# Six-layer cross network on one core: tail weights in one broadcast DMA per layer, first group loaded in half chunks with its tails on column tiles, late residual tile transposed in halves

## The chip, the cores and the metric

One core of one Trainium2 chip. Times are device microseconds of one execution. The time of a run is about 1.8 us more than the span of the profile of the same run (477.49 beside 475.7 for the kernel before). All runs told here fell in the fast state, with a granted TensorE clock of 0.994 to 1.000.

## The reference

```python
B, F, D, L = 16384, 26, 16, 6          # Din = 416
def reference(x0, ws, bs):
    x = x0
    for l in range(L):
        proj = jnp.einsum('bd,de->be', x, ws[l]) + bs[l]
        x = x0 * proj + x
    return x
```

x0 is 16384 x 416, ws is 6 x 416 x 416, all in bf16.

## The kernel before

The rows are worked on in eight groups (0 to 7) of 2048, with features on partitions. 416 features are three tiles of 128 and a tail of 32. A group is four chunks of 512 rows; the tails of its four chunks are stacked into one tile of 128 partitions, and their product with the 32 tail rows of a weight matrix is done by row-tiled matmuls (L477 in the profiles), four of which run side by side: eight take 0.61 us at 22.78 in the profile before, eight whole-array ones 1.89 at 12.21. For that the 32 tail rows of each layer's weights lie four times in `w3[l]`.

Every operation goes through `add(engine, instruction, reads, writes, lane)`, which works out the semaphore waits. "sp" is SyncE, whose queue issues nearly all transfers.

```python
def load_w3(l, eng):                                  # tail rows of layer l, once per quarter
    for j in range(NJ):
        add(eng, lambda h, j=j: h.dma_start(w3[l][j * T32:(j + 1) * T32, :], ws[l, NT * P:D, :]), ...)

def load_group(g, between=lambda: None):
    ...
    turn(0)                                           # DMA transposes, one per tile of 128 features
    add("sp", lambda h: h.dma_start_transpose(Tb, x0[rows, D - P:D]), ...)   # the tails' columns
    turn(1)
    turn(2)
    between()                                         # group 1: weights of layer 1
    for j in range(NJ):                               # the "tail rows": four quarters of the tail tile
        add("sp", lambda h, q=q, j=j: h.dma_start(x0s[s][q, XW:XW + CH], Tb[P - T32:P, j * CH:(j + 1) * CH]), ...)
    ...

# ---- start of the SyncE queue
load_nat(0, 0, 2)                                     # group 0 comes row-major, TensorE transposes it
load_nat(0, 2, KK)
load_wm(0, "sp")
for j in range(1, NJ):
    load_nat(j, 0, KK)
load_w3(0, "sp")
load_group(1, lambda: load_wm(1, "sp"))
load_wm(2, "sp")
load_w3(2, "sp")

def transposed_chunk(j):                              # 12 transposes of the three tiles, 4 of the tail
    ...
    for n, (t, k) in enumerate(seq + [(NT, k) for k in range(KK)]):
        ...
        add("pe", lambda h, t=t, k=k, b=b, c=c: h.transpose(
            psum_t(b)[:, c], x0n[:, j, k, first[t]:first[t] + P], ident[:, :]), ...)
    ...                                               # copies out by ScalarE and VectorE

def first_job():
    ...
    transposed_chunk(1)
    transposed_chunk(2)
    full(g, l, 0, ba, True, True, chunks=[1])
    transposed_chunk(3)
    load_w3(1, "act")                                 # from ScalarE's queue
    full(g, l, 1, bb, True, True, chunks=[1])
    full(g, l, 0, ba, True, True, chunks=[2, 3])
    rows32(g, l, 0, ba, False)                        # the first row-tiled matmuls
    ...

def rest_turn(t):                                     # residual of the last layer, tile t, back to row-major
    add("sp", lambda h: h.dma_start_transpose(
        x5f[:, :, t * P:(t + 1) * P], xs[s][:, t * GC:(t + 1) * GC]), ...)
```

Group 7 is written row-major; its last stores, three of 416 KB, one of 208 KB from SyncE and one of 208 KB from ScalarE, end the kernel.

Of the kernel before, what the change touches and what calls it, by code (L numbers as in the profile page):

```python
# [3 lines left out]
P = 128  # L4
CH = 512
# [193 lines left out]
def bass_standalone__cross_network_dcn__recsys_kernel(  # L199
# [56 lines left out]
    def x0_tok(s, t, j):  # L256
        return ("x0", s, t, j)
# [21 lines left out]
    def load_wm(l, eng):  # L279
        add(eng, lambda h: h.dma_start(wm[l][:, :, :], ws[l, 0:NT * P, :].rearrange("(t p) f -> p t f", p=P)),  # L280
            writes=[("wm", l)], lane=f"wm{l}", batch=0)

    def load_w3(l, eng):
        for j in range(NJ):
            add(eng, lambda h, j=j: h.dma_start(w3[l][j * T32:(j + 1) * T32, :], ws[l, NT * P:D, :]),
                writes=[("w3", l, j)], lane=f"w3{l}", batch=0)

    def load_group(g, between=lambda: None):
        s = slot(g)
        rows = slice(g * GC, (g + 1) * GC)  # L290
        def turn(t):
            add("sp", lambda h: h.dma_start_transpose(
                x0s[s][:, t * GC:(t + 1) * GC], x0[rows, t * P:(t + 1) * P]),
                writes=[x0_tok(s, t, j) for j in range(NJ)], lane=f"x0_{s}_{t}", batch=g)

        turn(0)
        add("sp", lambda h: h.dma_start_transpose(Tb, x0[rows, D - P:D]),
            writes=[("ost", t, j) for t in range(NT + 1) for j in range(NJ)], lane="Tb", batch=g)
        turn(1)
        turn(2)  # L300
        between()
        for j in range(NJ):
            q = slice(j * T32, (j + 1) * T32)
            add("sp", lambda h, q=q, j=j: h.dma_start(x0s[s][q, XW:XW + CH], Tb[P - T32:P, j * CH:(j + 1) * CH]),
                reads=[("ost", 0, 0)], writes=[("x03q", s, j)], lane=f"x03_{s}", batch=g)

        if turn_of(g, 1):
            rotate(x0s[s][:, XW:XW + CH], x0s[s][:, XW + CH:XW + 2 * CH], turn_of(g, 1),
                   x03_toks(s), ("x03r", s), f"x03r_{s}", g)
# [210 lines left out]
    def load_nat(j, k0, k1):  # L520
        add("sp", lambda h: h.dma_start(x0n[:, j, k0:k1, :], perm(g0, j)[:, k0:k1, :]),  # L521
            writes=[("nat", j, k) for k in range(k0, k1)], lane=f"nat{j}{k0}", batch=0)
# [6 lines left out]
    load_nat(0, 2, KK)  # L529
    load_wm(0, "sp")  # L530
    for j in range(1, NJ):
        load_nat(j, 0, KK)
    load_w3(0, "sp")
    load_group(1, lambda: load_wm(1, "sp"))
    load_wm(2, "sp")
    load_w3(2, "sp")

# [8 lines left out]
    def psum_t(b):  # L546
        return psum[:, b * CH:(b + 1) * CH].bitcast(BF16)

    def transposed_chunk(j):
        ba, bb = ((0, 1), (3, 0), (1, 3), (0, 1))[j]  # L550
        s = slot(0)
        first = (0, P, 2 * P, D - P)
        seq = [(t, k) for t in range(NT) for k in range(KK)]
        if j == 0:
            seq = [(t, k) for k2 in (0, 2) for t in range(NT) for k in (k2, k2 + 1)]
        for n, (t, k) in enumerate(seq + [(NT, k) for k in range(KK)]):
            if j == 0 and n == NT * 2:
                keep_busy(2, 3)
            b, o = (ba, t * CH) if t < 2 else (bb, (t - 2) * CH)
            c = slice(o + k * P, o + (k + 1) * P)  # L560
            add("pe", lambda h, t=t, k=k, b=b, c=c: h.transpose(  # L561
                psum_t(b)[:, c], x0n[:, j, k, first[t]:first[t] + P], ident[:, :]),
                reads=[("nat", j, k), x0_tok(nat, 0, 0), "ident"], writes=[("ps", b)])
        for t in range(2):
            add("act", lambda h, t=t: h.activation(  # L565
                x0s[s][:, cols(t, j)], psum_t(ba)[:, t * CH:(t + 1) * CH], ACT_F.Copy),
                reads=[("ps", ba)], writes=[x0_tok(s, t, j)])
        add("dve", lambda h: h.tensor_copy(x0s[s][:, cols(2, j)], psum_t(bb)[:, 0:CH]),  # L568
            reads=[("ps", bb)], writes=[x0_tok(s, 2, j)])
        q = slice(j * T32, (j + 1) * T32)  # L570
        add("dve", lambda h: h.tensor_copy(x0s[s][q, XW:XW + CH], psum_t(bb)[P - T32:P, CH:2 * CH]),
            reads=[("ps", bb)], writes=[("x03q", s, j)])

    def first_job():

        g, l = 0, 0
        start_job(g, l)
        transposed_chunk(0)
        bt = 7
        for t in range(NT):  # L580
            add("pe", lambda h, t=t: h.transpose(
                psum_t(bt)[:, t * 8:t * 8 + L], brow[0:L, t * P:(t + 1) * P], ident[0:L, 0:L]),
                reads=["brow", "ident"], writes=[("ps", bt)])
        for j in range(NJ):
            q = slice(j * T32, (j + 1) * T32)
            add("pe", lambda h, j=j, q=q: h.matmul(
                psum_t(bt)[q, NT * 8:NT * 8 + L], brow[0:L, NT * P:D], ident[0:L, 0:L],
                is_transpose=True, tile_position=(0, j * T32)),
                reads=["brow", "ident"], writes=[("ps", bt)])
        add("act", lambda h: h.activation(  # L590
            bias[:, :, :], psum_t(bt)[:, 0:32].rearrange("p (t l) -> p t l", l=8)[:, :, 0:L], ACT_F.Copy),
            reads=[("ps", bt)], writes=["bias"])
        keep_busy(8, 3)
        ba, bb = [4, 5, 6, 7], [2, 3, 0, 1]
        full(g, l, 0, ba, True, True, chunks=[0])
        full(g, l, 1, bb, True, True, chunks=[0])
        transposed_chunk(1)
        transposed_chunk(2)
        full(g, l, 0, ba, True, True, chunks=[1])
        transposed_chunk(3)  # L600
        load_w3(1, "act")
        full(g, l, 1, bb, True, True, chunks=[1])
        full(g, l, 0, ba, True, True, chunks=[2, 3])
        rows32(g, l, 0, ba, False)
        evacuate(g, l, 0, ba, [0, 1], 2, vector=[2, 3])
        full(g, l, 1, bb, True, True, chunks=[2, 3])
        rows32(g, l, 1, bb, False)
        rows32(g, l, 2, ba, True)
        evacuate(g, l, 1, bb, list(range(NJ)), 2)
        full(g, l, 2, ba, False, True, lambda j: evacuate(g, l, 2, ba, [j], 1))  # L610
        finish_tile(g, l, NT)
        tails([(g, l)])
# [66 lines left out]
    def rest_turn(t):  # L679

        s = xset[(LAST, L - 1)]
        if t == 0:
            add("pool", lambda h: h.memset(warm[:, :], 0.0), writes=x0_all(s5) + x03_toks(s5) + ["x5 free"])
        add("sp", lambda h: h.dma_start_transpose(
            x5f[:, :, t * P:(t + 1) * P], xs[s][:, t * GC:(t + 1) * GC]),
            reads=[("x", s, t, j) for j in range(NJ)] + ["x5 free"],
            writes=[("x5n", j, t) for j in range(NJ)], lane=f"x5_{t}", batch=0)

    items = []
    where = {(b[min(1, len(b) - 1)], 0): b for b in batches[:-1]}  # L690
# [263 lines left out]
```

## Time and profile before

| | before |
|---|---|
| time, median of 3 runs | 477.13 us (476.96 to 477.26) |
| span of the profiled execution | 475.7 us (that execution took 477.49) |
| TensorE busy | 97% |
| granted clock | 0.999 |

How to read what the prediction shows: the first of its fences is the part "engines" of the page (busy us, share of the span, instructions) with the last line of the part "chain that ended last". The second is a timeline: start and length in us, engine, line, operation, output and inputs, shapes, count, and in brackets the idle time before the group with what released it. The third are waits: engine, output, line, releaser, then the total, the number and the longest.

### The profile page before, as it was taken

Reading aid. Unit: us, or ns where it says so; the run is one execution under the profiler, and the core shown is the slowest. Engines: PE = TensorE matmul, PEld = TensorE weight load, DVE = VectorE, ACT = ScalarE, POOL = GpSimd, SP = SyncE. Lnnn points to the kernel's source line nnn. Section 1 sums busy time; section 2 is a strip of 40 time slices with the busy share of each in tenths; the row PEclk is TensorE's granted clock in tenths of the full one; section 3 lists DMA queues with packets and bytes.
Section 4 is the critical chain, followed back from the end, with each engine's and each line's share of the span. In section 5 each row is a group of like instructions: output and inputs, shape, how many; then the busy total and the mean of one; then the engine's idle time right before and its main releaser. Section 6 shows DMA issues by size and latency. Waiting matters only on the chain.

```text
span 475.7 us, 8355 instructions
## 1 busy us (share of the span) xinstructions
PE 462.2 (97%) x3325; PEld 195.7 (41%) x3379; DVE 404.0 (85%) x696; ACT 342.4 (72%) x372; POOL 6.8 (1%) x15
## 2 busy tenths in 40 slices
PE   7999999999999999999999999999999999999995
PEld 6344444444444444444444444434444444444442
DVE  2888888888888888898889869988888888888896
ACT  4677777777777777777777777777777777777785
POOL 1000000000000000000000000000000000000000
PEclk9999999999999999999999999999999999999999
DMA  8866950640002397369308940990000039025899
GB/s 223 181 150 137 190 113 1 142 81 1 28 7 44 63 228 158 76 139 244 84 21 195 208 108 9 178 279 2 1 10 25 4 64 242 15 45 117 227 155 288
DMA packets 138363, 53.31 MB, mean 112 GB/s; under 512 B 112330, under 2 KB 137428, under 8 KB 138324
## 3 DMA queue, kind: packets, MB, share of 16 engines
q1 hardware_dynamic: 137848, 52.46, 49.2%
q8 instruction: 26, 0.43, 0.4%
q10 hardware_dynamic: 476, 0.32, 0.2%
q14 instruction: 13, 0.11, 0.1%
HBM read 5.97 MB, written 13.63 MB: 41 GB/s over the span
## 4 chain that ended last, share of the span: by engine, by line
PE 95%; issue 1%; DMA 1%; ACT 1%; DVE 1%; SPq 0%
PE ps L456 77%; PE ps L477 7%; PE ps L497 6%; PE ps L798 2%; DMA x<-in_x_dram 1%; PE ps L471 1%; ACT tw L394 1%; PE ps L561 1%; PE ps L488 1%; DVE x L864 0%; PE ps L809 0%; ACT x L852 0%; DVE x L858 0%; PE ps L841 0%; SPq L521 0%
## 5 line engine op out<-in xcount | busy, mean ns | idle before, releaser
L394 ACT ACTIVATE tw<-ps,bias 128x1024 bf16<-128x1024 f32 (+1 forms) x295 | 299.8, 1071 | 119.8 <-PE ps L477 80.7
L456 PE MATMUL ps<-x,wm 128*128 128x512 bf16 x1638 | 371.7, 379 | 5.8 <-issue 3.7
L456 PEld LDWEIGHTS ps<-x,wm 128*128 128x128 bf16 x1692 | 158.9, 98 | 213.5 <-issue 27.9
L403 DVE TENSOR_TENSOR tw<-tw,x 128x1024 bf16<-128x1024 bf16 (+1 forms) x285 | 192.3, 682 | 52.8 <-ACT tw L394 52.4
L408 DVE TENSOR_TENSOR x<-tw,x 128x1024 bf16<-128x1024 bf16 (+1 forms) x285 | 183.0, 682 | 0.0
L477 PE MATMUL ps<-x,w 32*128 32x512 bf16 x512 | 39.2, 379 | 0.0
L497 PE MATMUL ps<-x,wm 128*32 128x512 bf16 x564 | 33.0, 380 | 0.0
L434 ACT ACTIVATE ts<-ps,bias 128x512 bf16<-128x512 f32 x47 | 28.8, 701 | 0.0
L438 DVE TENSOR_TENSOR x<-ts,x 128x512 bf16<-128x512 bf16 x47 | 18.6, 417 | 3.7 <-DMA x<-x 3.6
L497 PEld LDWEIGHTS ps<-x,wm 128*32 128x32 bf16 x564 | 13.8, 96 | 17.6 <-issue 5.3
L477 PEld LDWEIGHTS ps<-x,w 32*128 32x128 bf16 x512 | 7.8, 92 | 27.6 <-issue 27.1
L436 DVE TENSOR_TENSOR ts<-ts,x 128x512 bf16<-128x512 bf16 x47 | 18.5, 417 | 0.0
L666 POOL COPY ost<-ot 128x512 bf16<-128x512 bf16 x6 | 5.4, 898 | 423.7 <-DMA ot<-x 423.7
L798 PE MATMUL ps<-wm,x 128*128 128x416 bf16 x48 | 9.5, 340 | 0.0
L852 ACT ACTIVATE x<-ps 128x416 bf16<-128x416 f32 x16 | 7.7, 533 | 2.0 <-PE ps L798 1.9
L568 DVE COPY x<-ps 128x512 bf16<-128x512 bf16 x4 | 1.7, 424 | 8.7 <-PE ps L561 8.7
L565 ACT ACTIVATE x<-ps 128x512 bf16<-128x512 bf16 x8 | 4.3, 594 | 5.6 <-PE ps L561 5.6
L798 PEld LDWEIGHTS ps<-wm,x 128*128 128x128 bf16 x48 | 4.3, 98 | 4.2 <-issue 1.0
L561 PE MATMUL ps<-ident,x 128*128 128x128 bf16 x64 | 4.6, 226 | 1.4 <-DMA x<-in_x_dram 0.9
L858 DVE TENSOR_TENSOR x<-x,x 128x832 bf16<-128x832 bf16 (+1 forms) x10 | 5.0, 504 | 1.1 <-ACT x L852 1.1
L488 PE MATMUL ps<-x,w 32*32 32x512 bf16 x188 | 5.9, 374 | 0.0
L471 PE MATMUL ps<-x,w 32*32 32x512 bf16 x208 | 5.6, 385 | 0.0
(38 smaller groups left out, 35.7 us busy)
## 6 DMA issues: line engine op xcount, KB each, us to landing
out_dram<-ost SPq DMA_DIRECT2D x6, 1664.0 KB, 7.1
x<-in_x_dram SPq DMA_DIRECT2D x7, 416.0 KB, 8.0
x<-x SPq DMA_DIRECT2D x24, 96.0 KB, 2.2
wm<-in_ws_dram SPq DMA_DIRECT2D x6, 312.0 KB, 3.7
out_dram<-ost SPq DMA_DIRECT2D x2, 832.0 KB, 6.7
x<-x SPq DMA_DIRECT2D x22, 64.0 KB, 2.0
out_dram<-x SPq DMA_DIRECT2D x3, 416.0 KB, 3.6
x<-ost SPq DMA_DIRECT2D x28, 32.0 KB, 2.2
```

The lines of the kernel that those rows point to most:

```text
L394: add("act", lambda h, a=a, w=w, b0=b0: h.activation(tw[r][:, a * CH:(a + w) * CH], psum[:, b0 * CH:(b0 + w) * CH], ACT_F.Identity, bias=b ...
L403: add("dve", lambda h, a=a, e=e: h.tensor_tensor(tw[r][:, a * CH:e * CH], tw[r][:, a * CH:e * CH], x0s[s0][:, i * GC + a * CH:i * GC + e * ...
L408: add("dve", lambda h, a=a, e=e: h.tensor_tensor(xs[so][:, i * GC + a * CH:i * GC + e * CH], tw[r][:, a * CH:e * CH], src(i, a, e), ALU.ad ...
L434: add("act", lambda h: h.activation(ts[r][:, :], bank(b), ACT_F.Identity, bias=bias[:, 3, l:l + 1], scale=1.0), reads=[("ps", b), "bias"], ...
L436: add("dve", lambda h: h.tensor_tensor(ts[r][:, :], ts[r][:, :], x03, ALU.mult), reads=[("ts", r)] + tok0, writes=[("ts", r)], release=True)
L438: add("dve", lambda h: h.tensor_tensor(x3s[so][:, :], ts[r][:, :], res, ALU.add), reads=[("ts", r)] + rtok, writes=[("x3", so), ("x3", so, ...
L456: add("pe", lambda h, t=t, j=j: h.matmul(bank(banks[j]), wm[l][:, t, ecols], src(t, j, j + 1), start=(first and t == 0), stop=(not first a ...
L471: add("pe", lambda h, q=q, j=j, r=r, c=c, o=o: h.matmul(psum[o, banks[j] * CH:(banks[j] + 1) * CH], w3[l][q, i * P + c * T32:i * P + (c + ...
L477: add("pe", lambda h, q=q, j=j, r=r: h.matmul(bank(banks[j]), w3[l][q, ecols], src[q, :], start=first, stop=not first, tile_position=(r * ...
L488: add("pe", lambda h, l=l, b=b, s3=s3, ri=ri, qi=qi, ro=ro, qo=qo: h.matmul(psum[qo, b * CH:(b + 1) * CH], w3[l][qi, NT * P:D], s3[qi, :], ...
L497: add("pe", lambda h, t=t, j=j, src=src, l=l, b=b, ro=ro, qo=qo: h.matmul(psum[qo, b * CH:(b + 1) * CH], wm[l][:, t, NT * P:D], src(t, j, ...
L798: add("pe", lambda h, t=t: h.matmul(bank(b, n=D), xcol(t, j, kk), wm[l][:, t, :], start=(first and t == 0), stop=(not first and t == NT - 1)),
```

## The change

The intent: fewer issues on the queues (one DMA for the tail weights of a layer instead of four), an earlier first row-tiled matmul (TensorE can start on half a chunk, and the tails of all four chunks are transposed by 16 small matmuls on column tiles instead of 16 whole ones), tail rows of group 1 ahead of layer 1's weights in the queue, and no wait for the late residual tile.

```diff
     def load_w3(l, eng):
-        for j in range(NJ):
-            add(eng, lambda h, j=j: h.dma_start(w3[l][j * T32:(j + 1) * T32, :], ws[l, NT * P:D, :]),
-                writes=[("w3", l, j)], lane=f"w3{l}", batch=0)
-
-    def load_group(g, between=lambda: None):
+        add(eng, lambda h: h.dma_start(
+            w3[l][:, :], ws[l, NT * P:D, :].partition_broadcast(NJ)),
+            writes=[("w3", l, j) for j in range(NJ)], lane=f"w3{l}", batch=0)
+
+    def load_group(g):
@@
         turn(2)
-        between()
         for j in range(NJ):
             ...                                  # tail rows, unchanged
+        if g == 1:
+            load_wm(1, "sp")
@@
     for j in range(1, NJ):
-        load_nat(j, 0, KK)
+        load_nat(j, 0, 2)
+        load_nat(j, 2, KK)
@@ transposed_chunk: tile loop by halves (k2 in 0, 2), without the tails; new:
+    def transposed_tails(b):
+        for k in range(KK):
+            for j in range(NJ):
+                o = slice(j * T32, (j + 1) * T32)
+                add("pe", lambda h, j=j, k=k, o=o: h.matmul(
+                    psum_t(b)[o, k * P:(k + 1) * P], x0n[:, j, k, NT * P:D], ident[:, :],
+                    is_transpose=True, tile_position=(0, j * T32)), ...)
+        add("dve", lambda h: h.tensor_copy(x0s[s][:, XW:XW + CH], psum_t(b)[:, 0:CH]), ...)
@@ first_job
-        keep_busy(8, 3)
+        keep_busy(5, 3)
         ...
         full(g, l, 0, ba, True, True, chunks=[1])
+        full(g, l, 1, bb, True, True, chunks=[1])
         transposed_chunk(3)
+        transposed_tails(7)
         load_w3(1, "act")
-        full(g, l, 1, bb, True, True, chunks=[1])
@@ rest_turn
+        for j0, j1 in ((0, NJ),) if t == 0 else ((0, 2), (2, NJ)):
             add("sp", lambda h, ...: h.dma_start_transpose(
-                x5f[:, :, t * P:(t + 1) * P], xs[s][:, t * GC:(t + 1) * GC]),
+                x5f[:, j0 * KK:j1 * KK, t * P:(t + 1) * P], xs[s][:, t * GC + j0 * CH:t * GC + j1 * CH]),
             ...
```

## The prediction

> **What bounds the kernel now.** I read the page first: engines, then the chain that ended last.
>
> ```profile
> PE 462.2 (97%) x3325; PEld 195.7 (41%) x3379; DVE 404.0 (85%) x696; ACT 342.4 (72%) x372; POOL 6.8 (1%) x15
> ...
> PE 95%; issue 1%; DMA 1%; ACT 1%; DVE 1%; SPq 0%
> ```
>
> TensorE is busy 97% of a 475.7 us span and 95% of the chain lies on it. A change that removes almost no TensorE work can win only where TensorE stands idle, or at the end, behind its last matmul. So next I asked for the timeline of TensorE alone, from the start (start us, length us, engine, line, operation, shapes, count, then idle time and releaser):
>
> ```profile
> 5.81 1.24 PE L456 MATMUL ps<-x,wm 128*128 128x512 bf16 x5 [0.25 <-ACT x L565]
> 7.92 1.07 PE L561 MATMUL ps<-ident,x 128*128 128x128 bf16 x16 [0.87 <-DMA x<-in_x_dram]
> 9.56 1.05 PE L561 MATMUL ps<-ident,x 128*128 128x128 bf16 x16 [0.57 <-DVE x L568]
> 10.45 0.81 PE L456 MATMUL ps<-x,wm 128*128 128x512 bf16 x3
> 11.10 1.06 PE L561 MATMUL ps<-ident,x 128*128 128x128 bf16 x16
> 12.21 1.89 PE L456 MATMUL ps<-x,wm 128*128 128x512 bf16 x8
> 14.03 0.40 PE L477 MATMUL ps<-x,w 32*128 32x512 bf16 x4
> ...
> 22.78 0.61 PE L477 MATMUL ps<-x,w 32*128 32x512 bf16 x8
> 23.32 5.35 PE L456 MATMUL ps<-x,wm 128*128 128x512 bf16 x24
> ```
>
> The two idle stretches worth having are here: 0.87 us before 7.92 and 0.57 us before 9.56. After 9.56 TensorE runs without a visible gap. The first wait is for chunk 1 of the input. The second is put down to a VectorE copy that ended at 9.45, but the sixteen completion marks of chunk 2's load say otherwise: fifteen are there by 7.55 us and the sixteenth at 9.42. The other chunks look alike: chunk 1 has fifteen by 6.51 and the last at 7.88, chunk 3 fifteen by 8.77 and the last at 10.41. One share of each load is 1.4 to 1.9 us behind the rest, so both waits are waits for one slow share.
>
> Then the waits, total, times and longest, for the two other places that the change touches:
>
> ```profile
> PEld ps L477 <- DMA x<-ost: 0.4, 1, 0.4
> ...
> DVE x L864 <- DMA x<-x: 0.3, 1, 0.3
> ```
>
> The first is the tail rows of group 1 at 22.78 us: their last completion mark is at 22.53, so they arrive just in time. The second is the addition at 464.49 us which waits for the late residual tile.
>
> **What the Trainium skill says.** "TensorEngine Tiling (Array Packing)", section "Tiling Modes", has it that four 128x32 column tiles work independently, and that changing the mode drains the engine. The trace agrees on the first: 24 column-tiled matmuls of 512 columns (L497) stand in the chain with 1.41 us, where 24 whole-array ones take 5.29. For the drain I read an estimate from eight row-tiled matmuls (L477) of 0.54 us in the chain: two groups of four at 0.22 are 0.44, so some 0.1 for the way in and out.
>
> "DMA: Bandwidth & Descriptors", section "Why a DMA increments its semaphore by 16 and not by 1", says that the engines of one transfer are the largest number up to 16 that divides the slowest dimension of both sides, and its "Rules for kernel authors" name a leading zero-stride broadcast of c copies as confined to c engines. The broadcast has 4 copies outermost, so the tail weights should run on 4 engines with 32 rows each, where the four old transfers had 16 engines with 2 rows each. No broadcast is in this trace.
>
> The same page, "Queues, rings and completion order", has descriptors of one engine consumed in ring order. The trace fits it: three chunk loads of 8 packets per engine at 131 ns land about 1.05 us apart on the fifteen quick shares (6.51, 7.55, 8.77).
>
> **The change part by part.**
>
> Tail weights in one DMA. On the queue's timeline the four issues of layer 0 take 2.79 us (3.61 to 6.40), later sets 1.9 to 3.6. One issue costs some 0.5, so each layer saves 1.4 to 3 us of issuing. None lies on the chain: layer 0's tail weights have landed at 11.18 and are first used at 14.03. On four engines they are 32 packets of 39 ns (the median of an 832-byte packet), 1.25 us instead of 0.3. Behind the chunk loads of a quick engine (ended about 8.4) that is 9.7; behind the slow one (packets ended at 9.93) it is 11.2 and some 0.5 to land. Both are early enough. Gain on the path: 0.
>
> Half chunks. Chunks 1 to 3 come as two loads each. Packets shrink from 3328 to 1664 bytes, 131 ns to 69 ns each, so a chunk costs an engine 16 x 69 = 1.10 us instead of 1.05: later by 0.05 per chunk. The queue issues two more loads of about 0.43 us in place of each 0.48, 1.2 us in all, paid by the weights' 2.3. The use is that 6 of 12 transposes of a chunk can be done before its last half lands.
>
> Tails on column tiles. Of 64 whole-array transposes 16 go (4 per chunk), and 16 column-tiled ones come once. The last such group before, 16 small row-tiled transposes at 459.97 (L827), took 0.27 us; I take that. Four VectorE copies of 0.43 become one of 0.42; VectorE idles here, so that is no gain by itself.
>
> The sum, from the moment chunk 2 is complete (9.56) to the first row-tiled matmul (14.03). Before: 16 transposes 1.05, 3 matmuls 0.65, 16 transposes 0.89, 9 matmuls 1.95: 4.54, measured 4.47. After, with matmuls of 0.22 (5.29/24), transposes of 0.066 (1.05/16) in the first chunk and 0.056 (0.89/16) in the second: 6 transposes 0.40, 6 matmuls 1.32, 12 transposes 0.67, the tails 0.27 and 0.1 for the mode, 6 matmuls 1.32, together 4.08. With 0.1 for the smaller packets of two chunks the first row-tiled matmul starts at 9.66 + 4.08 = 13.74: 0.3 us earlier. The tails use the PSUM bank of the last chunk's accumulator; their copy ends near 12.9, the accumulator starts near 13.1: no wait, but close.
>
> What happens ahead of 9.56 counts for nothing so long as chunk 2's last half lands there. The shorter warm-up (5 instead of 8 dummy matmuls) and the quicker chunk 0 end some 0.5 us earlier in the wait for chunk 1.
>
> Weights of layer 1 after the tail rows of group 1. The four tail-row moves gain 0.6 us, the issue of the weights ahead of them (18.02 to 18.61). The weights then land some 2.5 us later, near 24.3; their first tile starts near 26.0. So this only guards the gain: without it tail rows at 22.53 would allow TensorE no more than 0.25 us.
>
> Late residual tile in halves. The first half can start when its own half of the sum is written, 0.65 us earlier. It removes the 0.3 us wait at 464.49. But VectorE then waits again: its next multiplication at 465.32 waits 0.24 us for ScalarE's eviction, and ScalarE follows TensorE. So 0 on the path.
>
> Sum: 0.3 us if the slow share stays as it is.
>
> **The rivals.**
>
> The slow share goes. It sits in loads of 3328-byte packets; in the loads of chunk 0, with 1664, all sixteen marks lie within 0.35 us. If the halves are without it, chunk 2 is complete near 7.8 and chunk 3 near 9.0 and TensorE's own work becomes the bound: about 2 us sooner at the first row-tiled matmul. Then the tail rows of group 1 bind: gained are 0.25 (their slack now), 0.6 (the order) and up to 0.5 from the earlier queue: 0.9 to 1.4 us. Against it speaks that three loads in a row had a slow share after the first, whatever made it. I give it one in three: 475.9.
>
> Four engines with 32 rows hold up group 1. Its transposes queue behind the tail weights. On the slow engine, 1.25 instead of 0.3 us would put the last transpose (landed 20.39) at about 21.4 and the tail rows, even reordered, near 23: 0.2 us later than now, and the gain is gone or slightly negative: 477.2. If the slow engine is none of the four (12 chances of 16), they are level with it and nothing is lost.
>
> The end matters. If the wait at 464.49 did travel to the last store it would give 0.3 more: 476.5 in the base case. The last multiplications and additions run back to back from 470.60, 6 us after that wait, with idle VectorE time between: I give it one in ten.
>
> **Range and chances.** Base 477.13 - 0.3 = 476.8 with weight 0.5; no slow share 475.9 with 0.35; lost gain 477.2 with 0.15. The mean is 0.5 x 476.8 + 0.35 x 475.9 + 0.15 x 477.2 = 476.5. The runs before spread 0.3, so I widen the outer cases: 475.6 to 477.3. Two per cent are 9.5 us; all idle time of TensorE is 13.5 us over the span and the change reaches under 3 us of it: faster 0.01, slower 0.01.
>
> **What the profile after will show.** Base case right: the first transposes of chunk 1 start before 7.9, those of chunk 2's last half near 9.5, the first row-tiled matmul near 13.7, and the shift of 0.3 stays to the end. The rival of the slow share: chunk 2 complete before 8.5 and a wait for the tail rows of group 1 near 21.5 to 22. The four engines: tail weights' landing time well over that of other loads, and TensorE waiting for group 1 between 20 and 23 us. The end: the addition's wait of 0.3 gone and its successor waiting for ScalarE some 0.3 longer. I would be wrong if the start is shorter by over 1.5 us, if the row-tiled matmul comes later than 14.03, or if the steady part between 60 and 440 us changes its length by more than 0.3.

## The result, and the profile after

| | before | after |
|---|---|---|
| time, median | 476.90 us (476.69 to 477.26, 6 runs) | 477.83 us (477.33 to 478.43, 6 runs) |
| ratio | | 1.0019, 95% [1.0006, 1.0032] |
| span | 475.7 | 475.5 |

A ratio here is of fast runs of the same rounds, and so not quite the ratio of the medians. Within 2% it is "the same", as expected, but it is a small loss where a gain of 0.6 us was predicted, and it lies above the predicted range. Over all, the kernel before has 48 runs with a mean of 477.23 and the changed one 17 with 477.88: 0.65 us slower.

The two traces alone would mislead. The profiled execution of before (477.49) was slower than all six of its timed runs above, that of after (477.33) the fastest of its own; so the spans show 0.2 us gained where the times show a loss. One has to go through the trace stretch by stretch.

The page of after: engines, and the end of the chain that ended last.

```profile
PE 462.6 (97%) x3322; PEld 195.5 (41%) x3376; DVE 402.9 (85%) x694; ACT 341.9 (72%) x371; POOL 6.4 (1%) x15
...
PE 92%; SPq 4%; issue 1%; ACT 1%; DVE 1%; DMA 0%
```

TensorE has the same work. SyncE's queue is now on the chain with 4%, where it had 0%: the chain goes back through transfers of group 1. The timeline of TensorE at the start of after:

```profile
5.81 1.46 PE L456 MATMUL ps<-x,wm 128*128 128x512 bf16 x5
7.20 2.11 PE L559 MATMUL ps<-ident,x 128*128 128x128 bf16 x24
9.15 1.46 PE L456 MATMUL ps<-x,wm 128*128 128x512 bf16 x6
10.44 0.83 PE L559 MATMUL ps<-ident,x 128*128 128x128 bf16 x12
11.21 0.41 PE L579 MATMUL ps<-ident,x 128*32 128x128 bf16 x16
11.77 1.27 PE L456 MATMUL ps<-x,wm 128*128 128x512 bf16 x5 [0.16 <-issue]
12.97 0.40 PE L477 MATMUL ps<-x,w 32*128 32x512 bf16 x4
...
21.95 0.61 PE L477 MATMUL ps<-x,w 32*128 32x512 bf16 x8 [0.16 <-DMA x<-ost]
```

The waits for chunks 1 and 2 are gone and the first row-tiled matmul starts at 12.97 instead of 14.03. The 16 column-tiled transposes (L579) take 0.41 us. The row-tiled matmul on group 1's tail rows starts at 21.95 instead of 22.78.

Now the end. Timeline of before: TensorE's last matmuls (whole-array ones; row-tiled ones end the job a moment later), VectorE's last addition, ScalarE's issue of the last store:

```profile
468.49 2.28 PE L798 MATMUL ps<-wm,x 128*128 128x416 bf16 x12
...
472.30 0.59 DVE L864 TENSOR_TENSOR x<-x,x 128x832 bf16<-128x832 bf16 x1
472.92 0.42 ACTq L871 DMA_DIRECT2D out_dram<-x  x1
```

And of after:

```profile
464.49 0.59 DVE L872 TENSOR_TENSOR x<-x,x 128x832 bf16<-128x832 bf16 x1 [0.64 <-ACT x L866]
...
467.67 2.28 PE L812 MATMUL ps<-wm,x 128*128 128x416 bf16 x12
...
471.47 0.59 DVE L878 TENSOR_TENSOR x<-x,x 128x832 bf16<-128x832 bf16 x1
472.09 0.43 ACTq L885 DMA_DIRECT2D out_dram<-x  x1
```

The lead of 0.83 us is whole at VectorE's last addition (471.47 against 472.30). But that addition ends at 472.06 and the span at 475.5, 3.44 us later; before it was 472.89 and 475.7, 2.80 us. So 0.64 us are lost after the last computation, in the stores. The DMA view of 462 to 474.5 us, about a microsecond short of the end, says what is new there. Rows of queues: packets, MB, share of 16 engines; rows of issues: count, KB each, median us from issue to landing. Before:

```profile
q1 hardware_dynamic: 5063, 3.48, 92.6%
q10 hardware_dynamic: 211, 0.18, 3.8%
...
out_dram<-x ACTq DMA_DIRECT2D x1, 208.0 KB, 2.3
```

After:

```profile
q1 hardware_dynamic: 4493, 3.33, 86.9%
q10 hardware_dynamic: 272, 0.21, 5.0%
q14 instruction: 1, 0.01, 0.2%
...
out_dram<-x SPq DMA_DIRECT2D x3, 416.0 KB, 4.5
out_dram<-x SPq DMA_DIRECT2D x1, 208.0 KB, 3.5
out_dram<-x ACTq DMA_DIRECT2D x1, 208.0 KB, 2.9
```

The last store takes 2.9 us instead of 2.3, and a queue 14 of kind "instruction" has one packet there. It has 8192 bytes and starts at 465.17. In every trace such packets appear when SyncE's queue reaches about its 80th and 208th instruction, and its 336th where there is one: 128 apart. (Queue 14 has 13 such packets in before and in after; the other eleven come when ScalarE or VectorE is near its 64th, 192nd and so on, also 128 apart. None of those falls after 454.1 in any trace but before_pad, which is stalled: 456.4. A packet of 16 KB on queue 8, near 461 us and 465 in before_pad, stands in every trace and so makes no difference between them.) 8192 bytes over 128 instructions are 64 bytes for one. SyncE has 229 instructions in before, so the packet comes 21 before the end, at 445.3 us, ahead of group 7's stores, the first of which is issued at 466.44. The change takes fifteen away (five layers' tail weights on this queue, three issues each), adds three half chunks and one half residual tile, and leaves 218: the packet comes ten before the end: 0.44 us before the first of group 7's stores is issued (465.61), with two earlier stores of 832 KB still under way.

The Trainium skill knows the pieces. "DMA: Bandwidth & Descriptors", section "Queues, rings and completion order", lists queue row 14 as internal to the runtime, refill among its uses. "Runtime: NRT & Kernel Launch", section "Instruction fetch mechanics", has each engine's instructions fetched ahead by the sequencer's own DMA queue, and calls the cost mostly hidden. The trace agrees that the fetch has a row of its own (the packets stand under queue 14, kind "instruction"); the cost is the question of the experiments.

### The profile page after: what moved, and what is told of

It is laid out like the page before. It is cut to its first block, busy times and chain, and to the rows that moved or that the text cites. A ratio compares the mean times of both kernels' runs of the same rounds, so it can differ in the third digit from the quotient of the medians.

```text
span 475.5 us, 8331 instructions
## 1 busy us (share of the span) xinstructions
PE 462.6 (97%) x3322; PEld 195.5 (41%) x3376; DVE 402.9 (85%) x694; ACT 341.9 (72%) x371; POOL 6.4 (1%) x15
## 4 chain that ended last, share of the span: by engine, by line
PE 92%; SPq 4%; issue 1%; ACT 1%; DVE 1%; DMA 0%
PE ps L456 75%; PE ps L477 7%; PE ps L497 6%; SPq L292 2%; PE ps L812 2%; PE ps L471 1%; ACT tw L394 1%; SPq L521 1%; SPq L297 1%; PE ps L488 0%; DMA x<-ost 0%; SPq L303 0%; DVE x L878 0%; PE ps L823 0%; ACT x L866 0%
```

## The experiments

**Theory.** Two things, of which neither is the work removed. (1) The instruction fetch, moved into the last stores by the smaller number of queue instructions, costs about 0.6 us. (2) At the start TensorE's gain is mostly given back, because group 1's transposed tiles and tail rows arrive hardly earlier.

**Rivals.** (a) The broadcast on few DMA engines is itself what costs, by delaying group 1. (b) The half-chunk loads or the column-tiled tails cost. (c) The late residual tile in halves costs at the end. (d) There is no loss, only scatter.

**How each trace is cut.** F is the start of the first row-tiled matmul on group 0; S that of the row-tiled matmul on group 1's tail rows. Between S and the last matmul TensorE takes 447.66 us in every trace but one, so the steady part is out of the argument. E is from the end of VectorE's last operation to the end of the span. Then span = S + the same 450.1 for all + E (450.1 is 447.66 and the 2.45 us by which VectorE ends later). S - F without any wait is 8.75 us.

| kernel | SyncE instr. | F | S - F | S | E | span | median us (runs) | ratio [95%] |
|---|---|---|---|---|---|---|---|---|
| before | 229 | 14.03 | 8.75 | 22.78 | 2.80 | 475.7 | | |
| after | 218 | 12.97 | 8.97 | 21.95 | 3.44 | 475.5 | 477.83 (6) | 1.0019 [1.0006, 1.0032] |
| after_again | 218 | 12.77 | 9.19 | 21.96 | 3.36 | 475.4 | 477.75 (6) | 1.0020 [1.0006, 1.0034] |
| only_w3 | 214 | 13.14 | 9.82 | 22.96 | 3.44 | 476.5 | 478.06 (5) | 1.0021 [1.0009, 1.0032] |
| only_late | 230 | 13.24 | 8.75 | 21.99 | 2.79 | 474.9 | 476.89 (5) | 0.9996 [0.9984, 1.0008] |
| only_first | 232 | 12.45 | 10.27 | 22.71 | 2.79 | 475.6 | 477.05 (5) | 0.9995 [0.9983, 1.0007] |
| after_pad | 229 | 12.94 | 9.59 | 22.53 | 2.83 | 475.5 | 477.46 (6) | 1.0004 [0.9992, 1.0016] |
| before_pad | 346 | 13.65 | 8.75 | 22.40 | 3.29 | 480.0 | 481.31 (6) | 1.0082 [1.0065, 1.0099] |
| only_order | 229 | 13.27 | 8.75 | 22.02 | 2.93 | 475.1 | 476.98 (6) | 0.9997 [0.9985, 1.0010] |
| after_pad_pool | 229 | 12.73 | 9.94 | 22.67 | 2.81 | 475.6 | 477.64 (6) | 1.0007 [0.9995, 1.0019] |
| before_spread | 346 | 14.12 | 8.75 | 22.87 | 3.33 | 476.3 | 477.57 (5) | 1.0011 [0.9998, 1.0024] |
| w3_pad | 229 | 14.86 | 9.07 | 23.93 | 2.80 | 476.8 | 477.59 (5) | 1.0006 [0.9993, 1.0020] |
| split_loads | 232 | 13.06 | 9.37 | 22.43 | 2.79 | 475.3 | 477.38 (5) | 1.0001 [0.9988, 1.0014] |
| column_tails | 230 | 13.72 | 8.75 | 22.47 | 2.79 | 475.4 | 477.52 (5) | 1.0001 [0.9988, 1.0014] |
| late_w1 | 229 | 12.57 | 8.96 | 21.53 | 2.84 | 474.5 | 476.45 (5) | 0.9981 [0.9968, 0.9994] |
| late_w1_four | 237 | 13.00 | 9.43 | 22.43 | 2.80 | 475.3 | 476.83 (5) | 0.9993 [0.9981, 1.0006] |
| after_third | 218 | 12.55 | 9.68 | 22.24 | 3.38 | 475.7 | 477.68 (5) | 1.0008 [0.9996, 1.0020] |
| after_pad_2 | 229 | 13.00 | 9.36 | 22.36 | 2.84 | 475.3 | 477.06 (6) | 1.0001 [0.9987, 1.0015] |

Each group of four below ran on one chip and shares its runs of the kernel before. All sixteen gave correct results.

### First four: the change again, and its parts

**after_again** is the changed kernel unaltered.

> The changed kernel unaltered, for a second trace and a second comparison. Two traces so far: the first row-tiled matmul moved from 14.03 to 12.97 us and 0.83 us of that reaches the last matmul, but the last stores land late, one of sixteen shares 0.6 to 0.9 us behind the others, and an 8 KB instruction packet at 465.17 stands in their midst, where the kernel before has none after 452.64. Theory 1 (a slow share of the last stores eats the gain): time 0.5 to 1.0 us over before, and in this trace again one share of the last three stores 0.5 us or more behind, TensorE's last matmul some 0.8 us earlier than in before. Theory 2 (the trace of before was taken in an execution with a slow share at the start, typical ones have none, so the start gained nothing): time over before by the same, but the last stores' shares lie within 0.3 us. Chance: within 0.2 us of before.

Measured: 477.75 us, 1.0020. The loss repeats on another chip; rival (d) is weak from here on. E is 3.36 and the instruction packet lies among the last stores again.

**only_w3**: the kernel before with nothing but the broadcast.

```diff
-        for j in range(NJ):
-            add(eng, lambda h, j=j: h.dma_start(w3[l][j * T32:(j + 1) * T32, :], ws[l, NT * P:D, :]), ...)
+        add(eng, lambda h: h.dma_start(w3[l][:, :], ws[l, NT * P:D, :].partition_broadcast(NJ)), ...)
```

> The kernel before with the tail weights of each layer in one broadcast transfer and nothing else. Its SyncE queue has 15 transfers fewer. Theory 1 (fewer instructions on that queue move its instruction fetch into the last stores): 0.3 to 0.9 us slower than before, an 8 KB instruction packet after 460 us and one share of the last stores 0.5 us or more behind. Rival A (four engines with 32 rows each hold up group 1): slower by 0.2 to 0.9 us with TensorE waiting between 20 and 24 us, last stores even. If it is neither: within 0.2 us of before.

Measured: 478.06, 1.0021. The broadcast alone brings the whole loss, and both kinds of it: E is 3.44, and TensorE waits 1.00 us for group 1's tail rows. Timeline of TensorE in only_w3:

```profile
22.96 0.61 PE L477 MATMUL ps<-x,w 32*128 32x512 bf16 x8 [1.00 <-DMA x<-ost]
```

Its DMA view of 462 to 474.5 us:

```profile
q14 instruction: 1, 0.01, 0.2%
...
out_dram<-x ACTq DMA_DIRECT2D x1, 208.0 KB, 2.9
```

With 214 instructions the packet comes six before the end, at 473.8 us. That the broadcast runs on four engines is borne out by its semaphore: it gets five updates, where the four old transfers give 64, sixteen each. Five are too few for sixteen engines with one mark each, and fit four with one update more for the rest (the trace keeps the times of updates, not their size).

**only_late**: the kernel before with the residual tile in halves, the last hunk of the diff.

> The kernel before with the late residual tile transposed in halves and nothing else. One transfer more on the SyncE queue. Theory 1: within 0.2 us of before, no instruction packet among the last stores beyond that of before. Rival B (the halves disturb the stores that follow them): 0.4 to 1.0 us slower with the last stores landing late.

Measured: 476.89, 0.9996 with an interval on both sides of 1. The halves do neither good nor harm that these runs can tell, and E is 2.79: rival (c) falls. A by-product: this kernel's start is that of before, yet its F is 13.24, 0.8 earlier. So F of the first trace was not typical.

**only_first**: the changed kernel with the four transfers and the whole residual tile of before put back; what remains is the start (half chunks, column tiles, order).

```diff
     def load_w3(l, eng):     # as in the kernel before
@@ rest_turn
-        for j0, j1 in ((0, NJ),) if t == 0 else ((0, 2), (2, NJ)):
+        (one transpose of the whole tile, as in the kernel before)
```

> The kernel before with the first group's part alone: half chunks, tails on column tiles, the weights of layer 1 after the tail rows; four transfers of tail weights and the whole late tile as before. Theory 1: the start's gain survives, 0.5 to 1.0 us faster than before, last stores even. Theory 2 (typical executions of before have no slow share at the start): within 0.3 us of before. Rival A and B together: faster by 0.5 to 1.0 as well.

Measured: 477.05, 0.9995. No loss without the broadcast, so rival (b) is no cause of it; but the gain of 0.5 to 1.0 us that was expected is not there either, though F is the earliest of all, 12.45. The timeline shows where it goes:

```profile
12.45 0.39 PE L477 MATMUL ps<-x,w 32*128 32x512 bf16 x4
...
22.71 0.61 PE L477 MATMUL ps<-x,w 32*128 32x512 bf16 x8 [0.75 <-DMA x<-ost]
```

S is 10.27 after F, 1.52 more than TensorE needs. Of these, 0.75 are the wait shown for the tail rows; the rest are waits before it in the same stretch.

### Second four: move the instruction packet and nothing else

If the packet's place is what costs at the end, instructions that do nothing must move the cost. A semaphore that nobody waits for is incremented on SyncE's queue, in the middle of the kernel (during group 2's layer 4).

**after_pad**: the changed kernel plus 11 increments, 229 instructions as before.

```diff
+        if (g, l) == (2, 4):
+            for _ in range(11):
+                add("sp", lambda h: h.sem_inc(pr.padsem))
```

> The changed kernel with 11 semaphore increments that nobody waits for added to the SyncE queue in mid run (before job (2,4)), so that the queue again has 229 instructions before its end, as in the kernel before. In all six traces so far an 8 KB instruction packet appears when the queue reaches its 208th instruction: at about 445 us where there are four transfers of tail weights per layer, at 465.1 and 473.8 where there is one. And from the first row-tiled matmul on group 1's tail rows to the end it is 452.9 us in the former, 453.5 in the latter. Theory 1 (the packet among the last stores makes one DMA share of them late by 0.6): the packet returns to about 445, the last stores' shares lie within 0.3 us, the stretch is 452.9, and the time is 0.4 to 0.8 us under the changed kernel, about 477.2. Rival C (the broadcast itself or the halves of the late tile make the end late): stretch 453.5, time unchanged at 477.7 to 477.9.

Measured: E falls from 3.44 to 2.83, with the packet at 450.0. The time is 477.46, 1.0004 and so no longer told from before; the interval still overlaps that of after. F gained as in after, but S is 22.53: group 1 was late in this trace, with the last transpose at 21.12 and the tail rows at 22.48.

**before_pad**: the kernel before plus 117 increments in the same place: 346 instructions, so that a third packet comes ten before the end.

> The inverse: the kernel before with 117 such increments in mid run, so that its SyncE queue fetches once more, ten instructions before its end as in the changed kernel. No transfer and no arithmetic differs from the kernel before. Theory 1: an 8 KB packet among the last stores at about 465, one share of the last stores 0.5 us or more late, stretch 453.5, time 0.4 to 0.8 us over before. Rival C: packet or not, the stores stay even, stretch 452.9, time within 0.2 us of before.

Measured: 481.31, 1.0082. It says little as a time, for the increments had a side effect: they held SyncE's queue for some 7 us near 231 to 240 us, VectorE waited for rotated tail rows behind them, and TensorE took 451.85 us from S to the last matmul instead of 447.66. The waits of before_pad (total, times, longest):

```profile
DVE x L439 <- DMA x<-x: 18.4, 3, 12.9
```

That one wait is a flaw of the experiment. The end is still readable: the third packet is at 469.4, and E is 3.29.

**only_order**: the kernel before with layer 1's weights after the tail rows.

```diff
         turn(2)
-        between()
         for j in range(NJ):
             ...
+        between()
```

> The kernel before with the weights of layer 1 issued after group 1's tail rows and nothing else. The tail rows should land 0.6 us earlier. Theory 3 (what the start gains or loses is only the moment at which group 1's tail rows are there; TensorE itself reaches them near 22.0 in executions without a slow share): 0.1 to 0.5 us faster than before, the matmul on the tail rows between 21.9 and 22.1, stretch 452.9. If it is the slower first job that binds: within 0.1 us.

Measured: 476.98, 0.9997: no effect that can be told. Its tail rows land at 21.41, the earliest of all, but F is 13.27 and TensorE reaches S only at 22.02 by its own work. The order does guard, as long as TensorE is the later one.

**after_pad_pool**: after_pad with 15 increments, and group 1's four tail-row moves issued from GpSimd, to take them out of SyncE's line.

```diff
-            add("sp", lambda h, q=q, j=j: h.dma_start(x0s[s][q, XW:XW + CH], ...), ..., lane=f"x03_{s}", ...)
+            add("pool" if g == 1 else "sp", lambda h, q=q, j=j: h.dma_start(x0s[s][q, XW:XW + CH], ...), ...)
```

> The changed kernel with 15 increments on the SyncE queue (229 instructions again) and the four tail-row moves of group 1 issued from GpSimd's queue as soon as the tail columns are there, instead of behind the last transpose on SyncE's. If theory 3 holds and the tail rows then land before 21.5, TensorE waits for nothing at that place: the matmul on the tail rows at 21.5 to 21.7, stretch 452.9, span near 474.5 and time near 476.3, 0.6 to 1.0 us under before. If GpSimd's issue is slow, the tail rows land later than 22 and the time is 477.2 or more. If theory 3 is wrong the matmul comes earlier but the stretch grows by as much.

Measured: 477.64, 1.0007: nothing gained. The moves were issued from 16.90 to 19.00, but landed only at 22.19, and in this trace the last of group 1's transposes was the wait:

```profile
21.70 1.04 PE L457 MATMUL ps<-x,wm 128*128 128x512 bf16 x4 [1.01 <-DMA x<-in_x_dram]
```

So in this trace the issue of the tail rows is not what bounds group 1. Whether the moves, which now run beside the last transpose, made that one land late (21.65) is not shown.

### Third four: the packet brought into the old kernel, and the start's parts one by one

**before_spread**: before_pad mended. The same 117 increments, but spread over thirty jobs, at most four in one place.

```diff
+        if 0 < g < 7 and l > 0:
+            for _ in range(1 if (g, l) == (1, 1) else 4):
+                add("sp", lambda h: h.sem_inc(pr.padsem))
```

> The inverse again, without the side effect: in the earlier one, 117 increments in one place held the SyncE queue up in mid run and TensorE lost 4.2 us there. Now four (once, one) at the start of each of 30 jobs, 117 in all, so that the queue again fetches ten instructions before its end, and the stretch from group 1's tail-row matmul to the last matmul should stay 447.66 us. Theory 1 (an 8 KB instruction packet among the last stores makes them late): packet near 465, one share of the last stores 0.45 us or more late, 3.3 to 3.5 us from VectorE's last operation to the end in place of 2.8, time 0.4 to 0.8 us over before. Rival C: 2.8 and within 0.2 us of before.

Measured: the steady part is 447.66 again, S is 22.87 as in before (22.78), and E is 3.33 instead of 2.80. The packet is at 465.9. The time is 477.57, 1.0011, whose interval just includes 1. Its DMA view of 462 to 474.5 us:

```profile
q1 hardware_dynamic: 5062, 3.47, 92.7%
q14 instruction: 1, 0.01, 0.2%
...
out_dram<-x ACTq DMA_DIRECT2D x1, 208.0 KB, 2.8
```

The stores move the same bytes as before's (5062 packets to 5063). The old kernel has got the new kernel's end by instructions that do nothing.

How a packet of 0.3 to 0.4 us on one of the queues makes the stores later can be seen from their sixteen completion marks. How far the last mark of a store is behind the fifteenth, for the last five stores in order, in us:

```
before          .31 .23 .01 .01 .04    packet at 445.3
only_late       .17 .26 .03 .05 .04
only_order      .32 .25 .13 .15 .14
after_pad       .28 .36 .04 .04 .01    packet at 450.0
only_w3         .31 .23 .21 .52 .63    packet at 473.8
after           .89 .95 .57 .59 .63    packet at 465.17
after_again     .87 .96 .51 .52 .54    packet at 465.1
before_pad      .74 .81 .45 .47 .49    packet at 469.4
before_spread   .75 .84 .52 .53 .54    packet at 465.9
```

From the packet on, one share of sixteen is about half a microsecond or more behind the rest; without it the last mark of each of the last three stores is within 0.06 us of the fifteenth in all twelve traces but only_order, whose 0.13 to 0.15 go with the longest E of the twelve (2.93). In only_w3, where the packet comes latest, the first two stores still look like before's. The kernel ends with the slowest share: the last store of before has fifteen marks by 475.17 and the last at 475.20, that of after fifteen by 474.38 and the last at 475.00. The packets of the stores (832 bytes) say the same: in the six traces with the packet the last ten end one by one, over 0.36 to 0.38 us; in the twelve others they end close together, over 0.07 to 0.14 us. So one share alone still has data to move when the rest are done.

**w3_pad**: only_w3 plus 15 increments, 229 instructions.

```diff
+        if (g, l) == (2, 4):
+            for _ in range(15):
+                add("sp", lambda h: h.sem_inc(pr.padsem))
```

> The broadcast of the tail weights alone, with 15 increments so that the queue has its 229 instructions: its effect without the instruction fetch. Without the padding it cost 1.0 us. Theory 1 and rival A as two separate costs: the end is even again (2.8 us from VectorE's last operation), and what is left is later tail rows of group 1 (matmul between 22.4 and 23.0 us): 0.2 to 0.6 us over before. If the fetch was all of it: within 0.15 us of before.

Measured: E is 2.80 again, and the time 477.59, 1.0006, against 1.0021 of only_w3; the intervals overlap. S is 23.93, the latest of all, with F at 14.86 and tail rows at 23.88: this trace had a slow start, and its execution was the slowest of five (478.64).

**split_loads**: the kernel before with the half-chunk loads alone.

```diff
-        load_nat(j, 0, KK)
+        load_nat(j, 0, 2)
+        load_nat(j, 2, KK)
```

> The kernel before with chunks 1 to 3 loaded as two transfers each and nothing else; the transposes stay in their old order. Theory 4 (more issues on the SyncE queue delay group 1's transposes and tail rows): the queue's first transpose of group 1 issued near 7.3 instead of 6.2, tail-row matmul 0.2 to 0.7 later than 22.0, time 0.1 to 0.6 over before. If the transposes are bound by the data alone: within 0.15 us.

Measured: 477.38, 1.0001. F is 13.06, S - F 9.37: TensorE waits 0.6 us for group 1 on the way, whose tail rows land at 22.39. What F gains against 13.66 (the mean of the unchanged starts, below) is not kept to S.

**column_tails**: the changed kernel with the four transfers and whole chunk loads of before, so the column tiles (with the order, the shorter warm-up and the late halves) alone.

```diff
     def load_w3(l, eng):     # as in the kernel before
@@
-        load_nat(j, 0, 2)
-        load_nat(j, 2, KK)
+        load_nat(j, 0, KK)
```

> A version that may beat both: the changed kernel with four transfers of tail weights per layer and whole chunk loads, thus keeping the tails on column tiles, the order of the weights of layer 1, the shorter warm-up and the halves of the late tile. Theory 3 (the tail rows of group 1 and TensorE's first job are both at about 22.0, so both must be made earlier): tail rows land near 21.4 as with the order alone, first row-tiled matmul near 12.7, tail-row matmul at 21.4 to 21.7, even end, 0.3 to 0.7 us under before (476.4 to 476.8). If the group's transposes land late again, as with the half chunks: within 0.2 us.

Measured: 477.52, 1.0001, where 476.4 to 476.8 was hoped for. F is 13.72, S - F the bare 8.75. No part of the start, alone, moves the time measurably.

### Fourth four: what makes group 1 late, and a version that repairs both ends

In before and after, layer 1's tail weights are issued from ScalarE's queue near 11 to 12 us, beside SyncE's transposes of group 1. In SyncE's queue of after (with the line of ScalarE's below it) the transposes run from 5.81 to 18.03 and the tail rows start at 18.07:

```profile
13.23 4.80 SPq L292 DMA_TRANSPOSE x<-in_x_dram  x2
18.07 2.54 SPq L303 DMA_DIRECT2D x<-ost  x4
```

```profile
11.21 0.65 ACTq L284 DMA_DIRECT2D w<-in_ws_dram  x1
```

**late_w1**: the changed kernel with those weights taken off ScalarE's queue and issued by SyncE after layer 1's weights, and ten increments to keep the instruction packet out of the stores.

```diff
         if g == 1:
             load_wm(1, "sp")
+            load_w3(1, "sp")
@@ first_job
-        load_w3(1, "act")
@@
+        if (g, l) == (2, 4):
+            for _ in range(10):
+                add("sp", lambda h: h.sem_inc(pr.padsem))
```

> The changed kernel padded to 229 instructions, with the tail weights of layer 1 issued on SyncE's queue after the weights of layer 1 instead of on ScalarE's at 11 us, where they run beside group 1's transposes. In the traces so far TensorE needs 8.75 us from its first row-tiled matmul to that on group 1's tail rows if it waits for nothing; the kernels with whole chunk loads and four transfers take 8.75, the changed one 8.98 and 9.21, padded 9.59. Theory 5 (group 1's load is bound by the transfers that run beside it): tail rows land near 21.3, the interval is 8.75 to 8.9, the tail-row matmul at 21.5 to 21.8, time 0.3 to 0.8 us under before. If the load does not come earlier: interval 9.2 or more, time within 0.3 us of before.

Measured: 476.45 (476.31 to 476.64, five runs), 0.9981 [0.9968, 0.9994]. It beats both kernels. SyncE's queue in late_w1:

```profile
13.19 4.42 SPq L293 DMA_TRANSPOSE x<-in_x_dram  x2
17.65 2.54 SPq L304 DMA_DIRECT2D x<-ost  x4
...
20.87 0.63 SPq L285 DMA_DIRECT2D w<-in_ws_dram  x1
```

The last transpose lands at 19.74 instead of 20.48 to 21.65 in the other traces of the changed start, the tail columns at 15.42 instead of 16.2 to 16.9, the tail rows at 21.48. Timeline of TensorE:

```profile
12.57 0.40 PE L479 MATMUL ps<-x,w 32*128 32x512 bf16 x4
...
21.53 0.61 PE L479 MATMUL ps<-x,w 32*128 32x512 bf16 x8
```

S is 21.53, the earliest of all, and E 2.84.

**late_w1_four**: the same place for layer 1's tail weights, but four transfers for every layer, without increments (237 instructions keep the packet away).

> The same with four transfers of tail weights per layer and no padding: no transfer confined to four engines. Theory 5: as the other, 0.3 to 0.8 us under before, interval 8.75 to 8.9. If it is the broadcast that makes group 1's load late, this one is 0.2 us or more ahead of the other; if both stay level with before, what binds is neither.

Measured: 476.83, 0.9993: not told from before. S is 22.43 and S - F 9.43, where 8.75 to 8.9 was expected: the theory that group 1's load is bound by the transfers beside it missed here, for the last transpose lands at 21.09 although layer 1's tail weights are out of its way. With three more issues for layer 0 ahead of it, the first transpose of group 1 is issued at 7.36 instead of 6.21, and the tail rows land at 22.38. So rival (a) in its strict form, that running on four engines is what costs, is not borne out: given its place, the broadcast is at least level with the four transfers. That what it saves in issuing is the reason fits, but one trace of each does not show it.

**after_third** and **after_pad_2** repeat the changed kernel, without and with the 11 increments, side by side on one chip.

> The changed kernel unaltered, on the same chip as its padded version in this call: 0.6 to 1.0 us over before, stretch from the tail-row matmul to the end 453.5, instruction packet at 465.

> The changed kernel with 11 increments, again, for the difference to the unaltered one on the same chip: 0.5 to 0.7 us below it, stretch 452.9, no instruction packet after 455 other than the 16 KB one near 461.

Measured: 477.68 (1.0008) without and 477.06 (1.0001) with; E 3.38 and 2.84. In the trace the difference is again 0.54; in the times it is 0.3 to 0.6 and would not be told apart by itself. The unaltered kernel was expected 0.6 to 1.0 us over before and came out 0.35 over. after_pad_2's DMA view of 462 to 474.5 us, without a row for queue 14:

```profile
q1 hardware_dynamic: 4492, 3.33, 86.5%
q10 hardware_dynamic: 272, 0.21, 5.0%
...
out_dram<-x ACTq DMA_DIRECT2D x1, 208.0 KB, 2.3
```

### What the sixteen say together

The end: six traces have the packet among the last stores (after, after_again, after_third, only_w3, before_spread, before_pad), and their E is 3.29 to 3.44. The twelve others (before among them) have 2.79 to 2.93. It goes both ways: increments take it out of the changed kernel (after_pad, after_pad_2, w3_pad) and put it into the old one (before_spread, before_pad). In the times, the five with it (before_pad left out for its stall) have ratios from 1.0008 to 1.0021, the eleven changed ones without from 0.9981 to 1.0007. In the traces that is shown; the times agree, but no pair of kernels that differ in increments alone is told apart by its intervals. What is not settled is why a packet of 0.3 to 0.4 us on one queue delays a share by 0.5 to 0.9 us, and does so for stores issued well after it.

The start: five traces with the start of before (before, only_late, only_order, before_spread, before_pad) have F at 13.66 and S at 22.41 in the mean; five with the whole changed start (after, after_again, after_third, after_pad, after_pad_2) have 12.85 and 22.21. Of 0.8 us gained at F, 0.2 are left at S. S scatters by 0.9 us among kernels of one start, so the 0.2 are not to be leaned on. In the first set TensorE goes from F to S in exactly 8.75; in the second it waits 0.2 to 0.9 us on the way, for group 1's transfers. Which of the transfers before them is to blame is not shown: moving one of them out of the way (late_w1) went with 0.9 us at S against the padded kernels' mean of 22.45, in one trace, with five runs that agree within 0.33 us; but the same move with four transfers per layer (late_w1_four) left S at 22.43. So late_w1 is a version that is faster than before and after; what makes it so stays open.

Together: -0.2 at S and +0.6 at E make +0.4, where the pooled times have +0.65. The rest lies within what single traces scatter.

## Why the prediction was right or wrong

**Right.** The late residual tile: the wait of 0.32 us at 464.49 is gone, VectorE's next wait for ScalarE grew from 0.24 to 0.64, and only_late has 0.9996; 0 on the path, as worked out. The weights' order only guards: only_order has 0.9997. The column-tiled tails: 0.27 and 0.1 for the mode were taken, 0.41 us is measured; a little by luck, since the 0.27 was read from transposes of 32 columns and these have 128. The broadcast on four engines: five updates of its semaphore fit it. The steady part: 447.66 us on both sides.

**Right in mechanism, off in size.** The first row-tiled matmul was put at 13.74 and came at 12.97, in the mean 12.85. (A slip beside it: three more chunk loads are issued, not two; split_loads has 232 instructions to 229. And the quick shares land 1.04 and 1.22 us apart, not both about 1.05.) The prediction's base case kept the slow share as it was; in after it has shrunk (the first half of chunk 1 has fifteen shares at 6.38 and the last at 7.15, 0.8 behind instead of 1.4). So the rival "the slow share goes" was the truer one up to here, including its next sentence: "Then the tail rows of group 1 bind".

**Wrong: "Base 477.13 - 0.3 = 476.8".** The gain at the start was counted from one trace, whose 1.4 to 1.9 us of slow shares were read as a feature of the kernel. Unchanged starts had F between 13.24 and 14.12 in five traces; in only_late the chunks were complete at 6.87, 8.19 and 9.48 where they had been at 7.88, 9.42 and 10.41. So the first trace's F is at the late end of what one start gives: their mean is 13.66, 0.4 earlier, without any change.

**Wrong: the step from the first row-tiled matmul to the end.** The base case said that the shift "stays to the end". It holds only while group 1's transfers are ahead of TensorE. The prediction's own numbers had 0.25 us of slack and up to 0.6 and 0.5 more from the order and the queue; of those the tail rows, which had landed at 22.53 and were to come about a microsecond sooner, landed at 21.90 to 22.48 in the changed kernels. The rival "Four engines hold up group 1", with weight 0.15, saw the place but not the reason; only_w3's wait of 1.00 us is its case, late_w1 against late_w1_four its limit.

**Wrong: "Gain on the path: 0" for the tail weights in one DMA.** This is the larger mistake. It weighed when the issues happen and when the weights land, and did not count the instructions themselves. Eleven fewer on SyncE's queue shift an instruction fetch from 445 us into the last stores, and E goes from 2.80 to 3.44. The rival "The end matters" looked at the end for the wait of a residual tile, and gave it one in ten; the stores behind the last addition were taken as fixed. No view that the prediction read gives the size, but the DMA queues of the page list the instruction packets, and their times in the trace of before show that they come at fixed counts.

The two mistakes cancel the gain: what remained of 0.8 us at the start was 0.2, and 0.6 was lost at the end.

## What to carry to other kernels

Before you trust a gain of under a microsecond, follow it stretch by stretch to the last store, and take the baseline from more than one trace. A change in the number of instructions on a queue moves the places where its instructions are fetched; look where such a packet falls, and if it falls among the last stores, add or move a few idle instructions (0.5 to 0.6 us here). When the front of a kernel gets faster, look first at the transfers of the next stage, and try to take what isn't needed yet off their way (late_w1: 476.45 us, against 477.06 of after_pad_2 on the same chip, also without the packet in the stores; a few runs, with intervals that just overlap, and a cause that is not shown).

## What the Trainium skill lacked or had wrong

- "Runtime: NRT & Kernel Launch", section "Instruction fetch mechanics", gives refills of 16 KiB, 256 instructions. That fits queue 8 (26 packets of 16 KB in before, beside TensorE's 6723 instructions). On SyncE the runs show packets of 8192 bytes, 128 instructions apart (about the 80th, 208th and 336th).
- The same section counts the cost of a fetch as mostly hidden. For the engine's own stream no run here tells; for the stores that share the DMA engines it did not: one share of each remaining store was 0.5 to 0.9 us later than the rest, and the kernel ended 0.5 to 0.6 us later (E of 3.29 to 3.44 against 2.79 to 2.93). No page has that cost.
- "DMA: Bandwidth & Descriptors", "Rules for kernel authors", on the leading broadcast confined to as many engines as copies: agreed (five semaphore updates instead of 64). What it lacks is the other side: one issue of 0.73 us instead of four of 2.79 went with the earlier start of group 1 here (late_w1 with S at 21.53, late_w1_four with 22.43; one trace each).
- No page explains, for the hardware queues used here, why one share of some loads with packets of 3328 bytes lands 1.4 to 1.9 us late in one execution and not in another (chunk 1 complete at 7.88 in one trace, at 6.87 in another, with the same loads).
